# Nine output products two steps earlier, and two of the last four stores from ScalarE

## The chip, the cores and the metric

One of the eight cores of a Trainium2 chip runs the whole kernel. A core has five engines that run at the same time and wait for each other through semaphores: TensorE (PE: matrix products into PSUM, its weight loads shown apart as PEld), VectorE (DVE), ScalarE (ACT), GpSimd (POOL) and SyncE (SP, which here only issues DMA transfers). The metric is the device time of one execution in microseconds (us), as the median of several runs. A profiled execution is timed too; its span runs from its first to its last instruction.

## The reference

The kernel computes a normalised attention block, gated by a small dense network, with a residual:

```
xn = layernorm(x)                       # x: 2048 x 512
s  = attention(xn; wq, wk, wv, wo)      # 32 heads of 16, one shared key and value head
g  = silu(mish(xn @ w1 + b1) @ w2)      # inner width 1792
out = x + s * g

attention: q = xn @ wq, k = xn @ wk, v = xn @ wv
           p = softmax(q k^T / 4);  s = concat_heads(p v) @ wo
```

The part that matters here is the last one: `s` is the product of the heads' outputs (2048 x 512) with `wo` (512 x 512), which is multiplied by `g`, added to `x` and stored.

## The kernel before

**Tiling.** The 2048 rows are cut in 4 chunks of 512. The 32 heads are taken in groups of 4, so there are 8 groups to a chunk and 32 units in all. A unit walks over the 2048 keys in 16 tiles of 128, one tile to a step, so the kernel has NS = 512 steps. In a step TensorE makes four score products (`e`, line 1040, one for each head of the group: 128 keys x 512 rows), ScalarE takes the exponential of each out of PSUM (`pts`, line 1045), and TensorE multiplies those of two steps before with the values (`pv`, line 1127; four to a step, each shown as two instructions in the profile), all into one PSUM bank for the unit. Row maxima of the scores (`m`, lines 1069 and 1073, reduced by VectorE) run 22 steps ahead and end before the stretch that matters here. The products of the dense network and of the projections are slipped in between (`xps`).

**Output products.** For a chunk and a row tile `tt` (0 to 3, 128 rows each) the product with `wo` is a group of 12 matrix products: four tiles of 128 head columns, and three terms for each (high by high, high by low, low by high: numbers are split in two parts for precision). `Group`, `begin`, `finish` and `fill` handle such a group: `begin` takes the first one of the queue that is ready and gives it a PSUM bank, and `fill(n)` issues up to n of its products. In the last chunk each group is cut in two by `wo_groups`: the first 9 products need the head columns 0 to 383 alone, the last 3 need the columns of the last two units. The first parts of row tiles 0, 1 and 2 become ready 16 steps before the end and are issued in the steps from `NS - LEAD` to `NS - 2`, which `tail_block` writes in pairs. The first part of row tile 3 becomes ready at step NS.

**The end.** The main loop writes steps 510 and 511 in this order: four `e`, then `fill(4, ...)`, then the `pv` of step s - 2. At s = NS it writes the `pv` of steps 510 and 511 and calls `o_last`. That function copies the last unit's result out of PSUM (`os`, half by ScalarE on line 1190, half by VectorE on line 1191), turns it with four small products (`low` and `otop`, lines 1197 and 1198), divides by the softmax sums (`sc` on ScalarE, `oc` on VectorE) and writes the last head columns as high and low part into `ot_all`, in two halves: the first half (row tiles 0 and 1) by VectorE, the second (row tiles 2 and 3) by ScalarE on line 1206 and GpSimd. It calls `fill(2, True)` between the copies and the turns, and `fill(7, True)` behind the turns. Then come the four second parts of 3 products each. `post` multiplies each row tile by the gate (`y` or `wop`, VectorE, line 169) and adds `x` (`xr`: GpSimd for row tiles 0 and 1, VectorE for 2 and 3, once all four have been multiplied). `store` issues the 256 KB row tile to memory (line 919).

**Banks.** PSUM has 8 banks of 128 x 512. The pool `ps_e` has three of them, `ps_m` three, `ps_v` one and `ps_x` one. In the last six steps three of the four `e` of a step live in `ps_e` and one in `ps_m`; the PSUM tile of row tile 3 (`wop3`) lives in `ps_e` too. A tile of a pool waits until the bank that it takes over has been read.

The lines that set when the last row tile's first part starts, and where it is issued:

```
first.append(Group(mms[:9], ..., [lambda: NS - (16, 16, 16, 0)[tt], lambda: ot_done.get((c, 2))], ...))
...
for i in range(4):
    e_one(s, i)
fill(4, cur["g"] is not None and cur["g"].alloc is not None)
```

Of the kernel before, what the change touches and what calls it, by code (L numbers as in the profile page):

```python
# [122 lines left out]
def block_kernel(ctx: ExitStack, tc: tile.TileContext, x, wq, wk, wv, wo, w1, b1, w2, out):  # L123
# [10 lines left out]
    pe, act, dve, pool, sp = nc.tensor, nc.scalar, nc.vector, nc.gpsimd, nc.sync  # L134
# [18 lines left out]
    def sp_at(us):  # L153

        sp_t[0] = max(sp_t[0], us_of(step[0])) + us
        return step_of(sp_t[0] + 2.6) - 1

    def pool_at(margin):
        t = step_of(busy[0]) + margin
        return max(t + 0.5 if lead else math.ceil(2 * t) / 2, step[0])  # L160
# [5 lines left out]
    def ew(eng, o, a, b, op):  # L166
        if eng is pool:
            charge(1.3)
        eng.tensor_tensor(out=o, in0=a, in1=b, op=op)  # L169
# [4 lines left out]
    def mul(eng, o, a, b):  # L174
        ew(eng, o, a, b, ALU.mult)
# [32 lines left out]
    outr = out.rearrange("o (t p) d -> (o t) p d", p=P)  # L208
# [24 lines left out]
    def stats(t):  # L233
        st = sb.tile([P, 6], F32, tag="st", name=f"st{t}")
        dve.bn_stats(st, xin[divmod(t, 4)])
        dve.bn_aggr(mvs[:, t], st)
# [153 lines left out]
    def at(s, fn):  # L390
        if s <= step[0]:
            fn()
        else:
            timed.setdefault(s, []).append(fn)
# [37 lines left out]
    def item(tag, key, src):  # L432
        i = Item(tag, key, src)
        items[tag].append(i)
        return i
# [210 lines left out]
    def mm12(lhs, rhs, n):  # L646
        res = []
        tot = 3 * n
        for j in range(n):
            for a, b in TERMS:  # L650
                res.append(Mm(pe, lambda j=j, a=a: lhs(j, a), lambda j=j, b=b: rhs(j, b), len(res), tot))
        return res
# [103 lines left out]
    def hold(hist):  # L756
        hist.append(None)
        n = len(hist) - 1

        def free():  # L760
            hist[n] = pool_at(0.1)
        return free
# [132 lines left out]
    ot_done = {}  # L895
# [3 lines left out]
    def wo_groups(c):  # L899
        last = c == NC - 1  # L900
        its = [item("wb", ("o", k), wo[P * k:P * (k + 1), :]) for k in range(4)]
        first, second = [], []
        adds = []

        def mk(tt):
            st = {}
            t = 4 * c + tt

            def pre():
                if xr_hist[-4] is None:  # L910
                    return False
                st["x"] = sb.tile([P, D], F32, tag="xr", name=f"xr{t}", bufs=4)
                st["free"] = hold(xr_hist)
                sp_at(0.5)
                sp.dma_start(st["x"], xr[t])
                return True

            def store():
                sp.dma_start(outr[t], st["x"])
                st["free"]()  # L920

            def post(ps):
                y = y_of[tt]
                wo_left[c] -= 1
                xx = st["x"]
                if last and tt > 1:
                    mul(dve, ps, ps, y)
                    adds.append(lambda: (ew(dve, xx, ps, xx, ALU.add), store()))
                    if tt == 3:
                        for add in adds:  # L930
                            add()
                    return
                mul(dve, y, ps, y)
                ew(pool, xx, xx, y, ALU.add)
                at(step[0] if last else pool_at(0.1), store)

            mms = mm12(lambda j, a: ot_of[c, j][:, a, P * tt:P * (tt + 1)],
                       lambda j, b: its[j].tile[:, b], 4)
            done = [lambda: ot_done.get((c, 3)), lambda: y_done.get((c, tt))]
            if not last:  # L940
                first.append(Group(mms, post, its, done, pre, wo=c))
                first[-1].dve = True
                return
            kept = {}

            def alloc():
                pool_, tag = ((ps_m, "m"), (ps_x, "x"), (ps_m, "m"), (ps_e, "e"))[tt]
                kept["ps"] = pool_.tile([P, D], F32, tag=tag, name=f"wop{tt}")
                return kept["ps"]
            first.append(Group(mms[:9], lambda ps: None, its, [lambda: NS - (16, 16, 16, 0)[tt], lambda: ot_done.get((c, 2))], wo=c, alloc=alloc))  # L950
            second.append(Group(mms[9:], post, its, done, pre, wo=c, alloc=lambda: kept["ps"]))
        for tt in range(4):
            mk(tt)
        return first + second
# [258 lines left out]
    NS = 16 * NU  # L1213
# [32 lines left out]
    def task(eng, us, fn, deps=(), **kw):  # L1246
        t = Task(eng, us, fn, deps, **kw)
        plan[eng].append(t)
        return t
# [53 lines left out]
    st = [task("DVE", 0.83, lambda t=t: stats(t), at=xat[t], prio=t // 4 * 2) for t in range(12)]  # L1303
# [368 lines left out]
```

## Time and profile before

| | |
|---|---|
| median of 3 runs | 1575.29 us (1574.7 to 1577.19) |
| profiled execution, its time | 1576.59 us |
| profiled execution, its span | 1574.8 us |
| granted TensorE clock, mean | 0.998 |
| busy: PE, DVE, ACT, POOL | 99%, 86%, 82%, 40% of the span |
| DMA queue that the kernel's transfers use | one (SP issues all of them) |

The busy share of TensorE is that of pipelined products whose ends are modelled, so 99% does not say that nothing more fits. The change touches only the last 20 us of the span, from about 1556 us on, and there the engines are far from evenly busy. Such a stretch is read from the order in time of each engine, not from shares.

### The profile page before, as it was taken

To read this page: it belongs to the slowest core of one execution; us is meant where nothing else is said; L and a number is where in the kernel's file an instruction comes from. 1 tells how busy PE (TensorE), PEld (TensorE's weight loads), DVE (VectorE), ACT (ScalarE), POOL (GpSimd) and SP (SyncE) were. 2 spreads that over 40 slices of the span, in tenths; PEclk is the share of its full clock that TensorE was granted. 3 is DMA by queue.
4 is the path that set the end of the run, shared out by engine and by line. 5 is a ranking of instruction groups with operands and counts; after the bars stand their busy time and mean duration, and the time that the engine had idled before them with its cause. 6 is when DMAs were issued, how large, how long until landed. Compare 5 with 4: busy or idle time off the path is not lost.

```text
span 1574.8 us, 31440 instructions
## 1 busy us (share of the span) xinstructions
PE 1560.2 (99%) x11738; PEld 881.1 (56%) x11738; DVE 1348.0 (86%) x2281; ACT 1291.4 (82%) x2502; POOL 636.9 (40%) x669
## 2 busy tenths in 40 slices
PE   9999999999999999999999999999999999999998
PEld 6555655655555565565555556556555555655644
DVE  6998888888989988888898988888889999888843
ACT  5589888788898778977989888897788978888785
POOL 4688249457257202431624422163152323315022
PEclk9999999999999999999999999999999999999999
DMA  6333133133151313203113220322321213031110
GB/s 185 108 125 118 37 103 135 49 112 118 29 158 62 98 27 112 71 18 103 53 46 121 91 92 17 103 68 81 99 59 53 85 58 116 16 98 32 61 36 27
DMA packets 74119, 125.21 MB, mean 80 GB/s; under 512 B 21536, under 2 KB 35648, under 8 KB 73968
## 3 DMA queue, kind: packets, MB, share of 16 engines
q1 hardware_dynamic: 73968, 123.21, 24.9%
q8 instruction: 93, 1.52, 0.4%
q14 instruction: 58, 0.48, 0.1%
HBM read 75.31 MB, written 26.21 MB: 64 GB/s over the span
## 4 chain that ended last, share of the span: by engine, by line
PE 96%; ACT 2%; DVE 1%; DMA 0%; POOL 0%; issue 0%; DVEq 0%; POOLq 0%; ACTq 0%
PE xps L116 43%; PE pv L1127 32%; PE m L1069 12%; PE e L1040 6%; PE xps L112 1%; ACT pts L1045 1%; DVE mb L1073 1%; PE warm L1293 1%; PE kp L335 1%; PE xp L294 0%; PE warm L1372 0%; PE wop L116 0%; DMA rawwb<-in_dram 0%; PE wop L112 0%; DMA ks<-ks 0%
## 5 line engine op out<-in xcount | busy, mean ns | idle before, releaser
L1073 DVE TENSOR_REDUCE mb<-m 128x1 f32<-128x512 f32 x2048 | 1265.8, 682 | 172.2 <-PE m L1069 127.0
L1045 ACT ACTIVATE pts<-e 128x512 f32<-128x512 f32 x2038 | 1060.9, 607 | 222.5 <-PE e L1040 156.2
L1069 PE MATMUL m<-ks,qt 48*128 48x512 f32 (+1 forms) x2048 | 841.8, 425 | 1.6 <-DMA ks<-ks 1.1
L1040 PE MATMUL e<-qt,ks 64*128 64x512 f32 x2048 | 750.1, 407 | 1.8 <-ACT pts L1045 1.5
L1127 PE MATMUL pv<-pts,vaug 128*32 128x512 f32 x4076 | 530.1, 603 | 0.0
L1069 PEld LDWEIGHTS m<-ks,qt 48*128 48x128 f32 (+1 forms) x2048 | 367.3, 185 | 108.1 <-DVE mb L1073 54.6
L1040 PEld LDWEIGHTS e<-qt,ks 64*128 64x128 f32 x2048 | 373.7, 186 | 25.3 <-ACT pts L1045 12.2
L116 PE MATMUL xps<-wbs,act 64*128 64x512 f32 x1248 | 315.3, 397 | 0.0
L116 PE MATMUL xps<-xt,ws 64*128 64x512 f32 x1128 | 313.1, 410 | 0.3 <-ACT pts L1045 0.3
L116 PEld LDWEIGHTS xps<-xt,ws 64*128 64x128 f32 x1128 | 194.5, 185 | 183.3 <-ACT pts L1045 121.4
L116 PEld LDWEIGHTS xps<-wbs,act 64*128 64x128 f32 x1248 | 225.8, 185 | 66.0 <-ACT pts L1045 32.7
L1127 PEld LDWEIGHTS pv<-pts,vaug 128*32 128x32 f32 x4076 | 88.1, 108 | 152.1 <-issue 144.1
L169 POOL TENSOR_TENSOR hb<-hb,t 128x512 f32<-128x512 f32 x56 | 72.1, 1288 | 162.3 <-ACT t L798 82.0
L179 POOL TENSOR_SCALAR t<-t 128x512 f32<-128x512 f32 x56 | 34.4, 615 | 180.2 <-ACT t L785 180.1
L116 PE MATMUL xps<-xt,wq 64*128 64x512 f32 x336 | 93.0, 409 | 0.0
L116 PEld LDWEIGHTS xps<-xt,wq 64*128 64x128 f32 x336 | 57.9, 185 | 55.1 <-ACT pts L1045 37.7
L169 POOL TENSOR_TENSOR oc<-oc,sc 128x512 f32<-128x512 f32 (+1 forms) x16 | 20.6, 1286 | 152.5 <-DMA qt<-qh 78.6
L116 PE MATMUL xps<-wbs,ot_all 64*128 64x512 f32 x288 | 79.5, 408 | 0.0
L116 PEld LDWEIGHTS xps<-wbs,ot_all 64*128 64x128 f32 x288 | 49.5, 184 | 46.7 <-ACT pts L1045 28.5
L169 POOL TENSOR_TENSOR act<-hb,act 128x512 fp32r<-128x512 f32 x56 | 72.2, 1289 | 4.7
L169 POOL TENSOR_TENSOR hb<-hb,u 128x512 f32<-128x512 f32 x56 | 72.2, 1289 | 4.4
L169 POOL TENSOR_TENSOR u<-u,t 128x512 f32<-128x512 f32 x56 | 71.9, 1284 | 4.7
(154 smaller groups left out, 908.6 us busy)
## 6 DMA issues: line engine op xcount, KB each, us to landing
wbs<-w SPq DMA_DIRECT2D x38, 512.0 KB
ws<-w SPq DMA_DIRECT2D x35, 512.0 KB
qt<-qh SPq DMA_DIRECT2D x256, 32.0 KB
w<-wbs SPq DMA_DIRECT2D x14, 512.0 KB
wq<-wq SPq DMA_DIRECT2D x14, 512.0 KB
wbs<-wo SPq DMA_DIRECT2D x12, 512.0 KB
w<-ws SPq DMA_DIRECT2D x11, 512.0 KB
rawws<-in_dram SPq DMA_DIRECT2D x21, 256.0 KB
```

What stands on the lines that cost most here:

```text
L112: self.pe.matmul(ps, self.lhs(), self.rhs(), start=(self.k == 0), stop=(self.k == self.tot - 1))
L116: i = self.pe.matmul(ps, self.lhs()[o], self.rhs()[o], start=(self.k == 0 and self.halves == 0), stop=(self.k == self.tot - 1 and self.hal ...
L169: eng.tensor_tensor(out=o, in0=a, in1=b, op=op)
L179: pool.tensor_scalar(o, o, lim, 0.0, op0=ALU.min, op1=ALU.max)
L335: pe.matmul(kp_of[c][o:o + HALF, 0:z.stop - z.start], w, x_[:, z], start=(dt + i == 0), stop=(dt == 3 and i == len(terms) - 1))
L1040: pe.matmul(e, ks[o:o + 64, P * k:P * (k + 1)], q[o:o + 64, p], start=True, stop=True)
L1045: x = act.activation(dst, e, AF.Exp, scale=0.25)
L1069: pe.matmul(m, q[o, p, P * t:P * (t + 1)], ks[o, C * kb:C * (kb + 1)], start=True, stop=True)
L1073: return dve.reduce_max(out=mb_of[v][:, kb, z:z + 1], in_=m, axis=AX.X)
L1127: pe.matmul(o[32 * j:32 * j + 32], vaug[:, k], pt, start=(k == 0), stop=(k == 15))
L1293: pe.matmul(warm, qts[0][:, 0, 0:P], qts[0][:, 0], start=True, stop=True)
```

## The change

Two numbers and one queue are changed. The first nine products of the last chunk's row tile 3 become ready at step NS - 2 instead of NS. The `fill(4, ...)` of steps 510 and 511 then finds them: it issues four in each, and the ninth is issued by `fill(2, True)` in `o_last`, whose `fill(7, True)` finds nothing any more. The PSUM bank of `wop3` is taken at step 510, behind that step's `e`. And of the last chunk's four stores, those of row tiles 1 and 3 are issued by ScalarE instead of SP.

```diff
             def store():
-                sp.dma_start(outr[t], st["x"])
+                (act if last and tt % 2 else sp).dma_start(outr[t], st["x"])
                 st["free"]()
...
-            first.append(Group(mms[:9], lambda ps: None, its, [lambda: NS - (16, 16, 16, 0)[tt], lambda: ot_done.get((c, 2))], wo=c, alloc=alloc))
+            first.append(Group(mms[:9], lambda ps: None, its, [lambda: NS - (16, 16, 16, 2)[tt], lambda: ot_done.get((c, 2))], wo=c, alloc=alloc))
```

On TensorE, from the last two `e` of step 510 to the end of the program (`e31_14_...` and `e31_15_...` are the scores of steps 510 and 511, `wop0` to `wop3` the row tiles' output products; `x4` counts instructions that read alike):

```order
 L1040 MATMUL e31_14_1_0_21223<-qt1_78,ks_92 128x512
 L1040 MATMUL e31_14_1_1_21226<-qt1_78,ks_92 128x512
+L112 MATMUL wop3_21229<-wbs_101,ot_all_103 128x512 x4
 L1127 MATMUL pv31_20975<-pts_102,vaug_94 32x512 x4
-L1040 MATMUL e31_15_0_0_21233<-qt1_78,ks_92 128x512
-L1040 MATMUL e31_15_0_1_21236<-qt1_78,ks_92 128x512
-L1040 MATMUL e31_15_1_0_21239<-qt1_78,ks_92 128x512
-L1040 MATMUL e31_15_1_1_21242<-qt1_78,ks_92 128x512
+L1040 MATMUL e31_15_0_0_21238<-qt1_78,ks_92 128x512
+L1040 MATMUL e31_15_0_1_21241<-qt1_78,ks_92 128x512
+L1040 MATMUL e31_15_1_0_21244<-qt1_78,ks_92 128x512
+L1040 MATMUL e31_15_1_1_21247<-qt1_78,ks_92 128x512
```

Four products of row tile 3 now stand between the scores of step 510 and the value products of step 508, and so ahead of the scores of step 511 as well; the scores themselves are the same instructions under new buffer numbers. The next piece of the same difference, on TensorE behind the scores of step 511:

```order
+L112 MATMUL wop3_21229<-wbs_101,ot_all_103 128x512 x4
 L1127 MATMUL pv31_20975<-pts_102,vaug_94 32x512 x12
-L112 MATMUL wop3_21261<-wbs_101,ot_all_103 128x512 x2
-L1197 MATMUL low0_21264<-os31_21257,turns_20929 64x256
-L1198 MATMUL otop0_21266<-os31_21257,turns_20929 64x256
-L1197 MATMUL low1_21265<-os2_21258,turns_20929 64x256
-L1198 MATMUL otop1_21267<-os2_21258,turns_20929 64x256
-L112 MATMUL wop3_21261<-wbs_101,ot_all_103 128x512 x7
+L112 MATMUL wop3_21229<-wbs_101,ot_all_103 128x512
+L1197 MATMUL low0_21271<-os31_21266,turns_20929 64x256
+L1198 MATMUL otop0_21273<-os31_21266,turns_20929 64x256
```

Another four stand ahead of the twelve value products of steps 509 to 511, one is left between them and the turns, and the seven behind the turns are gone, so that the second parts of the four row tiles follow the turns directly. On ScalarE, the end of its program in the changed kernel, with what each instruction waits for:

```order
L1202 ACTIVATE sc_20920<-sc_20920 64x256 [waits Activation_49]
L1201 ACTIVATE sc_20920<-low_21272 64x256 [waits PE_49]
L1202 ACTIVATE sc_20920<-sc_20920 64x256 [waits Activation_49]
L1206 ACTIVATE ot_all<-oc_20919 64x256 [waits DVE_49]
L919 DMA out_dram<-xr_20709 128x512 [waits Pool_49]
L919 DMA out_dram<-xr_20932 128x512 [waits DVE_49]
```

The two stores stand behind ScalarE's last computation; SP keeps those of row tiles 0 and 2.

## The prediction

> **What bounds the kernel now.** I read the page's head first, then the chain that ended last for the stretch that the diff touches, then TensorE, ScalarE, the other engines and the store queue in order of time.
>
> ```profile
> span 1574.8 us, 31440 instructions
> PE 96%; ACT 2%; DVE 1%; DMA 0%; POOL 0%; issue 0%; DVEq 0%; POOLq 0%; ACTq 0%
> ```
>
> TensorE carries the chain for nearly all of the span, so every product that is put in its way counts, unless TensorE would have waited there anyway. The change reaches only what lies behind the scores of step 510. There the chain runs:
>
> ```profile
> 1556.67 1.00 PE pv L1127 x8
> 1557.67 1.43 PE e L1040 x4
> 1559.10 2.71 PE pv L1127 x24
> ...
> 1564.40 2.50 PE wop L112 x10
> 1566.90 0.02 issue
> 1566.93 1.37 DVE y L169 x2
> ```
>
> The seven products of row tile 3 that stand behind the turns lie on it: of the ten `wop` from 1564.40, seven are theirs. So do the value products ahead of them. TensorE is therefore the bound on both sides of the move, and the question is at which place it has more idle time.
>
> **The old place.** TensorE, then the engines that make the last head columns:
>
> ```profile
> 1561.74 0.73 PE L112 MATMUL wop<-wbs,ot_all 128*128 128x512 f32 x2
> 1562.49 0.62 PE L1197 MATMUL low<-os,turns 128*64 128x256 f32 x2
> 1564.33 4.60 PE L112 MATMUL wop<-wbs,ot_all 128*128 128x512 f32 x19
> 1561.96 0.38 ACT L1190 ACTIVATE os<-pv 128x256 f32<-128x256 f32 x1 [1.45 <-PE pv L1127]
> 1564.46 0.29 DVE L1208 CAST ot_all<-oc 64x256 fp32r<-64x256 f32 x1
> 1564.78 0.42 DVE L169 TENSOR_TENSOR ot_all<-oc,ot_all 64x256 fp32r<-64x256 f32 x1
> 1565.58 0.41 ACT L1206 ACTIVATE ot_all<-oc 64x256 fp32r<-64x256 f32 x1 [0.75 <-DVE oc L169]
> 1566.14 0.73 POOL L169 TENSOR_TENSOR ot_all<-oc,ot_all 64x256 fp32r<-64x256 f32 x1 [19.46 <-ACT ot_all L1206]
> 1566.93 1.37 DVE L169 TENSOR_TENSOR y<-wop,y 128x512 f32<-128x512 f32 x2 [1.38 <-PE wop L112]
> ```
>
> The two products at 1561.74 lie beside the copy of `os`: the turns wait for its end (1562.34) and start at 1562.49. They cost nothing there. The seven of the x19 group do. Its spacing: a product that stands alone behind another kind takes 0.34 to the next (0.73 for two, less the 0.39 that the last one lasts), and the rest of the 4.60 is 17 gaps of 0.228. So the first product of row tile 0's second part started at 1564.33 + 0.34 + 6 x 0.228 = 1566.04. Its operands were there at 1564.75 (high part) and 1565.20 (low part, needed by its third product). TensorE was up to 1.2 us late.
>
> **What taking the seven away gives.** I keep the old times of the turns and shift everything later. Row tile 0: products at 1564.80, 1565.14, 1565.37. Its third came at 1566.49 and VectorE's product with the gate at 1566.93, 0.44 behind; now 1565.81. Row tile 1's third product follows 0.68 later. Row tile 2's third needs GpSimd's low part (1566.87), so it starts at 1566.92 and VectorE has it at 1567.36; row tile 3 follows 0.68 behind. So VectorE is ahead by 1.12 us at the start and by 0.93 at its third product (1568.29 before). Now the adds and the stores, in order of time and with the transfer engines' share:
>
> ```profile
> 1567.76 2.52 POOL L169 TENSOR_TENSOR xr<-xr,y 128x512 f32<-128x512 f32 x2 [0.89 <-DVE y L169]
> 1568.29 1.38 DVE L169 TENSOR_TENSOR wop<-wop,y 128x512 f32<-128x512 f32 x2
> 1569.58 1.28 DVE L169 TENSOR_TENSOR xr<-wop,xr 128x512 f32<-128x512 f32 x2
> 1569.09 2.04 SPq L919 DMA_DIRECT2D out_dram<-xr  x3
> 1570.31 0.82 SPq L919 DMA_DIRECT2D out_dram<-xr  x2
> 1570.74 0.88 SPq L919 DMA_DIRECT2D out_dram<-xr  x2
> 1571.00:1571.25 0.25, 0.00 (x0) 0.00 (x0) 0.00 (x0) 0.00 (x0) 0.00 (x0) 1.00 0.39 147
> 1571.25:1573.00 1.75, 0.00 (x0) 0.00 (x0) 0.00 (x0) 0.00 (x0) 0.00 (x0) 1.00 1.02 380
> 1573.00:1573.25 0.25, 0.00 (x0) 0.00 (x0) 0.00 (x0) 0.00 (x0) 0.00 (x0) 1.00 0.88 328
> 1573.25:1573.50 0.25, 0.00 (x0) 0.00 (x0) 0.00 (x0) 0.00 (x0) 0.00 (x0) 1.00 0.04 8
> ```
>
> In the last four rows the last two columns are the share of the DMA engines and GB/s. SP issues the second store at 1570.31, the third at 1570.74, the last at about 1571.2. Data of these three begin at 1571.15 (0.39 of a quarter before 1571.25), 0.84 behind the second store's issue, and run without a pause at share 1.02 to 1573.25: 2.10 us, 0.70 a store. So the end hangs on the start of the second store plus 2.10, not on SP's queue.
>
> Now: GpSimd is free at 1566.87, adds from 1566.93 to 1569.45 (2.52), and the second store goes out at 1569.48, 0.83 earlier than before. VectorE's adds start 1.29 behind its third product (1568.29 to 1569.58), at 1568.65, and end at 1569.33 and 1569.93. With two queues the third store can go out on SP at 1569.36, ahead of the second on ScalarE; data run from 1570.20 to 1572.30, 0.95 earlier than 1573.25; I take 0.93, VectorE's lead. On SP alone the order would be second, third, fourth, from 1569.48: 0.83. **The two stores on ScalarE are thus worth 0.10 us, the seven products 0.83.** No row here shows a transfer issued by ScalarE. The nearest are SP's, above all its first of all, issued at 0.74:
>
> ```profile
> 0.74 1.81 SPq L227 DMA_DIRECT2D pts<-in_dram  x4
> 1.60:1.80 0.20, 0.00 (x0) 0.00 (x0) 0.20 (x1) 0.20 (x1) 0.20 (x1) 1.00 0.17 41
> ```
>
> Its data began at about 1.77 (0.17 of 0.20 before 1.80), a lag of 1.03 instead of 0.84. With 1.03 ScalarE's second-tile store is ready at 1570.51, while the third still occupies the engines until 1570.90: free. Bounds: a gain of 0.10, and a loss of 0.19 if that longer lag ended up ahead of all three stores' data. I take the gain.
>
> The Trainium skill prices a transfer differently ("DMA: Bandwidth & Descriptors", section "Anatomy of one DMA", a fit made on transfers that GpSimd issues): about 2.0 us fixed plus bytes over 436 GB/s, so that each store would end on its own clock. By it the last store's issue (1571.2 before, 1569.96 now) would count and the gain be 1.24, the total 1576.7; the share of 1.02 above speaks for the engines being full instead.
>
> **The new place.** TensorE and ScalarE around steps 510 and 511:
>
> ```profile
> 1555.95 0.73 PE L1040 MATMUL e<-qt,ks 64*128 64x512 f32 x4
> 1556.61 1.06 PE L1127 MATMUL pv<-pts,vaug 128*32 128x512 f32 x8
> 1557.60 1.50 PE L1040 MATMUL e<-qt,ks 64*128 64x512 f32 x4
> 1559.03 2.78 PE L1127 MATMUL pv<-pts,vaug 128*32 128x512 f32 x24
> 1556.49 4.03 ACT L1045 ACTIVATE pts<-e 128x512 f32<-128x512 f32 x8 [0.64 <-PE e L1040]
> 1558.12 0.18 PEld L1040 LDWEIGHTS e<-qt,ks 64*128 64x128 f32 x1 [0.31 <-ACT pts L1045]
> 1558.60 0.18 PEld L1040 LDWEIGHTS e<-qt,ks 64*128 64x128 f32 x1 [0.30 <-ACT pts L1045]
> 1556.49 0.60 ACT L1045 ACTIVATE pts<-e 128x512 f32<-128x512 f32 x1 [0.64 <-PE e L1040]
> ```
>
> ScalarE's eight exponentials start every 0.49 us ((4.03 - 0.60) / 7), each done 0.60 behind its start. TensorE's third and fourth scores of step 511 wait for the banks that they free: the two PEld rows. That 0.61 is all the idle time that stands here, and eight products want 2 x (0.34 + 3 x 0.228) = 2.05 us. Step by step:
>
> 1. `wop3` takes the bank of step 510's first score, read at 1556.49 + 0.60 = 1557.09. TensorE stood ready for the value products at 1556.61; it now waits until 1557.14 (a bank's next user comes 0.05 behind: third exponential ends at 1558.07, score at 1558.12), and the value products wait in line behind it. Cost 0.53.
> 2. Four products: 1.02, to 1558.16.
> 3. The value products of step 508 as before, 0.99, then step 511's first two scores at 1559.15 instead of 1557.60. ScalarE has run dry at 1556.49 + 3 x 0.49 + 0.60 = 1558.56. Its next exponential starts 0.54 behind the scores (1555.95 to 1556.49), at 1559.69, and is done at 1560.29. With one of three banks held by `wop3`, the third score must take the bank of the first, so it waits until 1560.34, and the fourth behind it. Two scores take 0.33 (0.66 for four from 1555.95 to 1556.61): 1560.67. From first score to the next work that is 1.52, against 1.43 before (1557.60 to 1559.03): the old waits are not used as cover, since a longer one takes their place. Cost 0.09.
> 4. Four more products: 1.02, to 1561.69. The last exponential starts three times 0.49 or so behind 1559.69, and is done before the value products of step 511 need it at about 1563.5.
>
> The sum is 0.53 + 1.02 + 0.09 + 1.02 = **2.66 us later** for the twelve value products and all that follows. The ninth product fits beside the copy of `os`, as two did.
>
> **The total**: +2.66 - 0.83 - 0.10 = +1.73. The profiled execution had a span of 1574.8 and a time of 1576.59, 1.79 us more, and lay 1.30 above the median. On the median: 1575.29 + 1.73 = **1577.0 us**, on the span 1576.5. That is 0.11% slower, within the 0.2% (3.15 us) that about bounds what a measurement of this kernel tells from no change; the three runs themselves lie 2.5 us apart.
>
> **The rivals.**
>
> *Cover for the wait.* If the bank of `wop3` cost nothing, and the idle 0.61 took in as much of the moved products, they would cost 2.05 - 0.61 = 1.44, and the total 1575.29 + 1.44 - 0.93 = 1575.8. For it: two waits of that size are there. Against it: step 3, they only change their place. Chance 0.13.
>
> *All hidden, faster.* If ScalarE paced both steps, all eight products would be free: 1575.29 - 0.93 = 1574.4. Against it: ScalarE stands idle for 1.45 us ahead of `os`, waiting for TensorE (row at 1561.96). Chance 0.06.
>
> *The clock falls, slower.* The new order makes TensorE's work sparse: a wait of 1 us in step 511, then small turns, then a wait of 0.5 for the last head columns (1564.33 to 1564.80). If the granted clock halved there, the twelve last products would come at gaps of 0.68 and 0.456: the last third product at 1564.80 + 0.68 + 10 x 0.456 = 1570.04 instead of 1567.61, VectorE's last product with the gate at 1570.48, the last add 1.21 behind it (as from 1568.97 to the second add at 1570.18), 0.68 long, so to 1572.37, its store issued at 1572.40, data to 1573.94 instead of 1572.30. That is +1.64: 1578.7, just past 0.2%. The clock in the last column but two:
>
> ```profile
> 1573.50:1574.00 0.50, 0.00 (x0) 0.00 (x0) 0.00 (x0) 0.00 (x0) 0.00 (x0) 1.00 0.00 0
> 1574.00:1574.20 0.20, 0.00 (x0) 0.00 (x0) 0.00 (x0) 0.00 (x0) 0.00 (x0) 0.70 0.00 0
> ```
>
> It fell at about 1574.1, 5.1 us after the last product's end at 1568.93 (1564.33 + 4.60), so a pause of 1 us should not do it. The Trainium skill ("TensorE: Matmul & The Clock Gate", part 1) has the clock halved after an idle window of some 3.4 us that runs freely; the fall here agrees with that. It decides if the clock falls before the turns. Chance 0.03.
>
> *ScalarE's store is dear, slower.* The fourth store's data may begin as late as 1570.20 + 1.40 = 1571.60 without moving the end, a lag of 1.64 from its issue at 1569.96; each microsecond more adds one, and 3.1 us would pass 0.2%. No row comes near that: 1.03 is the longest. Chance 0.05.
>
> **How the numbers follow.** The forecast has 0.73. Its own spread is about 1 us either way, from the runs' 2.5 us and from the steps' ends: 2.66 without any gain gives 1578.0, and 1575.8 is the cover's case. One time in ten of it, and most of the two slow rivals, pass 1578.4: slower 0.12. Below 1572.1 no case ends; 0.02 for what I don't see. Same: 0.86. The range reaches from the forecast down past the cover's case and most of the hidden one, and up to the clock's: 1574.8 to 1578.9.
>
> **What would show it.** In the profile after: an idle wait of about 0.5 us ahead of the first `wop` at 1557.1; about 1 us between the second and third score of step 511, released by ScalarE; the value products' x24 group starting near 1561.7; no `wop` between the turns and the second parts; VectorE's first gate product about 1.5 us later than 1566.93; the three last stores' data again without a pause for 2.1 us; the last data at about 1575.0. I am wrong if the x24 group starts before 1561, if ScalarE's stores need more than 1.6 us to their data, or if the granted clock drops ahead of 1570.

## The result

The changed kernel took **1578.31 us** in the median of 12 runs (1575.4 to 1581.1), against 1574.9 us for the kernel before in 12 runs (1572.59 to 1577.19). The ratio is **1.0018, with a 95% interval of 1.001 to 1.0027**: slower by 1.6 to 4.3 us. The ratio itself lies within the 0.2%, the upper end of its interval past it, and the median lies inside the range forecast. The medians alone are 0.22% apart: five of the change's twelve executions had a mean granted clock of 0.999 or 1.0 and took 1575.4 to 1575.8 us, the seven others had 0.996 or 0.997 and took 1578.06 to 1581.1, so the median is one of the slower seven.

The profiled executions seem to say the opposite: the one after the change has a span of 1574.0 us, the one before 1574.8. The copies of each unit's result (line 1136, first and last start) show where these two part, first of the kernel before, then after the change:

```profile
L1136 ACT ACTIVATE os<-pv x31: 597/598/609, 138.4 to 1526.2; 128x512 f32<-128x512 f32 x31
```

```profile
L1136 ACT ACTIVATE os<-pv x31: 597/597/609, 135.6 to 1523.3; 128x512 f32<-128x512 f32 x31
```

The execution before the change is 2.8 us later at 138 us, and 2.9 us later at 1526: nothing is added in between, and the two programs are the same there. In the first 40 us its granted clock (last column but two) fell to half for some 7 us, which is 3.4 us of full clock:

```profile
26.00:28.00 2.00, 1.83 (x10) 0.76 (x10) 1.22 (x3) 1.76 (x3) 1.73 (x3) 0.96 0.50 170
28.00:34.00 6.00, 6.00 (x23) 2.84 (x20) 2.95 (x5) 3.39 (x11) 0.68 (x1) 0.50 0.53 173
34.00:36.00 2.00, 2.00 (x11) 1.22 (x9) 0.69 (x2) 0.99 (x5) 0.77 (x2) 0.83 0.19 48
```

That of the execution after the change stood at 1.00 in every 2 us from there to 50 us. So the spans can't be compared to 2 us, but the stretch that was changed can. From here on the **tail** is measured: from the first score of step 510 to the end of the span. The page gives a span to 0.1 us only; the trace holds it to the nanosecond (1574.771 before, 1574.009 after), and the tails below are taken from that. Before, it was 1574.77 - 1555.95 = 18.82 us. The expectations further down were written with the rounded spans, so they have 18.85 for it, 20.95 and +2.10 after the change, and 12.31 and 11.45 for the stretch from the first turn on.

TensorE after the change, in order of time:

```profile
1553.05 0.73 PE L1040 MATMUL e<-qt,ks 64*128 64x512 f32 x4
1554.24 1.20 PE L112 MATMUL wop<-wbs,ot_all 128*128 128x512 f32 x4 [0.46 <-ACT pts L1045]
1555.37 1.07 PE L1127 MATMUL pv<-pts,vaug 128*32 128x512 f32 x8
1556.36 0.49 PE L1040 MATMUL e<-qt,ks 64*128 64x512 f32 x2
1557.54 0.50 PE L1040 MATMUL e<-qt,ks 64*128 64x512 f32 x2 [0.68 <-ACT pts L1045]
1557.97 1.19 PE L112 MATMUL wop<-wbs,ot_all 128*128 128x512 f32 x4
1559.10 2.78 PE L1127 MATMUL pv<-pts,vaug 128*32 128x512 f32 x24
1562.55 0.62 PE L1197 MATMUL low<-os,turns 128*64 128x256 f32 x2 [0.24 <-ACT os L1190]
1564.96 3.24 PE L112 MATMUL wop<-wbs,ot_all 128*128 128x512 f32 x12 [0.50 <-DVE ot_all L1208]
```

The tail is 1574.01 - 1553.05 = **20.96 us, 2.14 more**. Both waits that were forecast stand there: the first four products wait for ScalarE's exponential (0.46 idle), and so does the third score of step 511 (0.68 idle, 1.18 behind the first). The 24 value products start 6.05 us behind the first score, where it was 3.08. From the first turn to the end of the span it is 1574.01 - 1562.55 = 11.46 us instead of 12.28: 0.82 come back there. ScalarE runs dry between the two steps:

```profile
1553.59 2.06 ACT L1045 ACTIVATE pts<-e 128x512 f32<-128x512 f32 x4 [0.64 <-PE e L1040]
1556.89 2.27 ACT L1045 ACTIVATE pts<-e 128x512 f32<-128x512 f32 x4 [1.24 <-PE e L1040]
```

Its eight exponentials, one unbroken row of 4.03 us before, are two rows with 1.24 us of waiting for TensorE between them. At the end, GpSimd's adds and the stores on both queues:

```profile
1567.02 2.51 POOL L169 TENSOR_TENSOR xr<-xr,y 128x512 f32<-128x512 f32 x2
1568.34 1.56 SPq L919 DMA_DIRECT2D out_dram<-xr  x2
1568.85 1.28 DVE L169 TENSOR_TENSOR xr<-wop,xr 128x512 f32<-128x512 f32 x2
1569.56 0.93 ACTq L919 DMA_DIRECT2D out_dram<-xr  x2
```

The store of row tile 2 on SP and that of row tile 1 on ScalarE, seen alone, and then the DMA engines' share (last column but one):

```profile
1569.55 0.34 SPq L919 DMA_DIRECT2D out_dram<-xr  x1
1569.56 0.39 ACTq L919 DMA_DIRECT2D out_dram<-xr  x1
```

```profile
1570.25:1570.50 0.25, 0.00 (x0) 0.00 (x0) 0.00 (x0) 0.00 (x0) 0.00 (x0) 1.00 0.39 147
1570.50:1572.25 1.75, 0.00 (x0) 0.00 (x0) 0.00 (x0) 0.00 (x0) 0.00 (x0) 1.00 1.02 382
1572.25:1572.50 0.25, 0.00 (x0) 0.00 (x0) 0.00 (x0) 0.00 (x0) 0.00 (x0) 1.00 0.86 320
```

The last three stores' data again run without a pause, from 1570.40 to 1572.47. The first of them are those of row tile 2, which SP issued at 1569.55, 0.85 us ahead. ScalarE's first store, issued at 1569.56, has its first data at 1570.73 by the packets of its queue in the trace, while those of SP's store still run.

### The profile page after: what moved, and what is told of

Same layout as the page of the kernel before. It is cut to its first block, busy times and chain, and to the rows that moved or that the text cites. A ratio compares the mean times of both kernels' runs of the same rounds, so it can differ in the third digit from the quotient of the medians.

```text
span 1574.0 us, 31438 instructions
## 1 busy us (share of the span) xinstructions
PE 1557.0 (99%) x11738; PEld 879.1 (56%) x11738; DVE 1347.9 (86%) x2281; ACT 1291.3 (82%) x2502; POOL 636.9 (40%) x669
## 4 chain that ended last, share of the span: by engine, by line
PE 96%; ACT 2%; DVE 1%; DMA 0%; issue 0%; POOL 0%; DVEq 0%; POOLq 0%; ACTq 0%
PE xps L116 43%; PE pv L1127 32%; PE m L1069 11%; PE e L1040 6%; ACT pts L1045 1%; PE xps L112 1%; DVE mb L1073 1%; PE warm L1293 1%; PE kp L335 0%; PE xp L294 0%; PE wop L112 0%; PE warm L1372 0%; DMA rawwb<-in_dram 0%; PE wop L116 0%; DMA ks<-ks 0%
```

## The experiments

The theory: a taken score bank and the products behind it delay the value products by 2.97 us; taking the products from behind the turns gives 0.82 back; ScalarE's stores are worth next to nothing. Rivals were put to each part. All are read by the tail, and by the **lead**, from the first score of step 510 to the first of the 24 value products. "No bank held" means no score bank.

| run | lead, us | first turn to end, us | tail, us |
|---|---|---|---|
| before | 3.08 | 12.28 | 18.82 |
| before, again | 3.09 | 12.29 | 18.83 |
| after | 6.05 | 11.46 | 20.96 |
| after, again | 6.05 | 11.45 | 20.96 |
| stores alone | 3.08 | 12.25 | 18.79 |
| products alone | 6.05 | 11.48 | 20.98 |
| all, no bank held | 4.59 | - | - |
| bank asked for early, nothing written, SP alone | 3.07 | 12.29 | 18.81 |
| one step later | 4.28 | 11.46 | 19.19 |
| one product early | 4.20 | 12.04 | 19.70 |
| one product early, no bank held | 3.08 | - | - |
| other order, two queues | 3.07 | 11.35 | 17.88 |
| other order, SP alone | 3.06 | 11.50 | 18.02 |

**Do the executions repeat?** The kernel before, and the one after, without an edit.

> The kernel before, unchanged, once more, to see how far two executions of one program differ, and where. The measure for all runs that follow is the tail: from the first score of step 510 to the end of the span. It was 18.85 us before (1555.95 to 1574.8) and 20.95 after the change (1553.05 to 1574.0). Theory: the tail is set by waits inside the core and comes out at 18.85 within 0.1; what differs between executions lies in the first 50 us, where the profile of before shows the granted clock at 0.50 for about 7 us and the one of after doesn't. Rival: the executions differ all along, then the tail is off by more than 0.3 and the change's +2.10 is not to be trusted.

> The changed kernel once more. Theory: its tail is 20.95 again within 0.1, with the value products at 6.05 and 11.45 from the first turn to the end, whatever the granted clock did in the first 100 us. Rival: the +2.10 was one execution's, then off by more than 0.3.

Both tails came out within 0.01 us of the first ones, and so did the pieces of them in the table. The spans were 1572.8 and 1573.0. The +2.14 (+2.13 between the second pair) is the change's, not an execution's.

**The stores alone.**

```diff
-                sp.dma_start(outr[t], st["x"])
+                (act if last and tt % 2 else sp).dma_start(outr[t], st["x"])
```

> The two stores alone go to ScalarE; the nine products stay where they were. Theory: the three last stores' data already run without a pause and start with the second store, which waits for GpSimd's add; the tail stays at 18.85, at most 0.1 shorter. Rival one: SP's queue of stores was the limit, then the last store is issued 0.3 us earlier (as soon as its add is done) and the tail is 18.5. Rival two: a first transfer from ScalarE is dear, then the tail is over 19.0.

The tail was 18.79, 0.03 to 0.04 shorter than in the two executions of before, and the time the same (ratio 1.0001, 0.9991 to 1.001). SP's queue was not the limit, and a store issued by ScalarE was not dear. The data of the last three stores in this run:

```profile
1566.75:1567.00 0.25, 0.00 (x0) 0.00 (x0) 0.00 (x0) 0.00 (x0) 0.00 (x0) 1.00 0.15 57
1567.00:1567.25 0.25, 0.00 (x0) 0.00 (x0) 0.00 (x0) 0.00 (x0) 0.00 (x0) 1.00 1.00 377
1567.25:1569.00 1.75, 0.00 (x0) 0.00 (x0) 0.00 (x0) 0.00 (x0) 0.00 (x0) 1.00 1.02 380
1569.00:1569.25 0.25, 0.00 (x0) 0.00 (x0) 0.00 (x0) 0.00 (x0) 0.00 (x0) 1.00 0.16 49
```

They take 2.08 us from the first byte to the last, against 2.10 before, whoever issues them.

**The products alone.**

```diff
-[lambda: NS - (16, 16, 16, 0)[tt], ...]
+[lambda: NS - (16, 16, 16, 2)[tt], ...]
```

> The nine products alone move; all four stores stay on SP. Theory: the tail is that of the whole change, 20.95 to 21.05, the value products of step 509 start 6.05 us behind the first score of step 510 (3.08 before), and the stretch from the first turn to the span's end is 11.45 to 11.55 (12.31 before). Rival: the stores on ScalarE gave a good part of that shorter stretch, then it is 11.7 or more and the tail over 21.2.

Tail 20.98, lead 6.05, 11.48 from the first turn on: the whole change, but for 0.02 us. The time was slower by 0.14% (ratio 1.0014, 1.0004 to 1.0024), 2.2 us. The two runs agree: the products make the change, the stores are worth 0.02 to 0.04 us.

**Bank or work?** The same move, but row tile 3 adds into row tile 2's bank, so the kernel no longer keeps the two apart.

```diff
+            if last and tt == 3:
+                mms[0].k = 1
+                mms[9].k = 0
...
+                if tt == 3:
+                    kept["ps"] = wops[2]
+                else:
+                    kept["ps"] = wops[tt] = pool_.tile([P, D], F32, tag=tag, name=f"wop{tt}")
```

> The whole change, but the nine moved products add into row tile 2's PSUM bank instead of taking one of the three score banks; row tiles 2 and 3 of the last chunk thus come out mixed, and the stretch behind the turns, where the two now wait for each other, is not to be compared. What counts is the start of the 24 value products behind step 511, as seen from step 510's first score: 3.08 us before, 6.05 after. Theory: of the 2.97 us the taken bank has about 1.4 (the wait ahead of the first four products and the wait of the third score), and the products 1.5 (2.26 us of work, less the 0.8 in which TensorE would have waited for banks): 4.6 us. Rival: the products cost all of it and the waits only show where TensorE would have stood anyway, then 6.0 again.

```profile
1552.39 0.73 PE L1047 MATMUL e<-qt,ks 64*128 64x512 f32 x4
1553.05 1.21 PE L112 MATMUL wop<-wbs,ot_all 128*128 128x512 f32 x4
1554.20 1.06 PE L1134 MATMUL pv<-pts,vaug 128*32 128x512 f32 x8
1555.19 0.73 PE L1047 MATMUL e<-qt,ks 64*128 64x512 f32 x4
1555.85 1.20 PE L112 MATMUL wop<-wbs,ot_all 128*128 128x512 f32 x4
1556.98 2.78 PE L1134 MATMUL pv<-pts,vaug 128*32 128x512 f32 x24
```

The lead is 4.59, as the theory had it: with a bank of its own out of the way, neither wait is left, and the four scores of step 511 go through in one piece. Of the 2.97 us, 1.46 belong to the bank and 1.51 to the eight products. The bank's part is more than the two waits of the change, because it also takes away cover: the scores of step 511 held TensorE for 1.43 us before (1557.60 to 1559.03), more than half of it waiting, and here for 0.66 (1555.19 to 1555.85), so 0.77 us of the products' work stands where TensorE would have waited; in the change the scores take 1.61 (1556.36 to 1557.97) in spite of the products.

**The bank alone.** This version asks for the bank at step 510 and issues no product there; all four stores are on SP.

```diff
-                fill(4, cur["g"] is not None and cur["g"].alloc is not None)
+                if s == NS - 2 and cur["g"] is None:
+                    begin()
```

> Row tile 3 takes its PSUM bank at step 510, as in the change, but all nine products stay at their old places. The bank's price alone, with no product behind which it could hide. Theory: the third score of step 511 waits for the first one's exponential, which ends 3.06 us behind step 510's first score, so it starts at 3.11 and the 24 value products at 3.54 instead of 3.08; the tail is 18.85 + 0.46 = 19.3. So the bank costs little by itself, and the 1.46 that it has in the change come from the products that push the scores, the exponentials and the third score behind one another. Rival: the bank alone already costs its 1.4 us: 4.5 and 20.3.

Lead 3.07, tail 18.81: nothing changed, and the theory's number was wrong. The edit did not do what it was for. In the built program the four scores of step 511 stand in banks 2, 0, 1 and 4, as before: `wop3` was asked for at bank 2, not written, and the bank was passed on. In the changed kernel `wop3` holds bank 2 and the scores stand in 0, 1, 0 and 4, so the third takes over the bank of the first, as the prediction's third step says. This run thus says nothing on the price of a held bank, and two more were made with one product each.

```diff
-                fill(4, cur["g"] is not None and cur["g"].alloc is not None)
+                if s == NS - 2:
+                    fill(1)
```

> The run that took the bank and issued no product changed no instruction's bank on the scores: a bank is held from the first write on. So now one product, the smallest that holds it: one of the nine at step 510, two beside the copy of the last result, six behind the turns; the stores are those of the change. Theory (a held bank makes waits): the product waits for its bank until 1.19 us behind step 510's first score (TensorE was ready at 0.66), holds TensorE for about 0.45, and the third score of step 511 waits for the exponential of the first, as that has only two banks left beside it; the 24 value products start at 4.25 instead of 3.08, so one moved product costs 1.2 us of the eight products' 2.97. Rival (cost by the product): 3.08 + 2.97 / 8 = 3.5.

> The same one product, but row tile 3 adds into row tile 2's bank (so row tiles 2 and 3 of the last chunk come out mixed, and the stretch behind the turns is not to be compared). Theory: no bank is held, the product fits into the 0.8 us for which TensorE would have waited in step 511, and the value products start at 3.1, as before. Rival: the wait in step 511 is not cover, then 3.5.

TensorE with one product in a bank of its own, and with one in row tile 2's bank:

```profile
1555.87 0.73 PE L1040 MATMUL e<-qt,ks 64*128 64x512 f32 x4
1557.05 0.50 PE L112 MATMUL wop<-wbs,ot_all 128*128 128x512 f32 x1 [0.45 <-ACT pts L1045]
1557.47 1.07 PE L1127 MATMUL pv<-pts,vaug 128*32 128x512 f32 x8
1558.47 0.49 PE L1040 MATMUL e<-qt,ks 64*128 64x512 f32 x2
1559.65 0.49 PE L1040 MATMUL e<-qt,ks 64*128 64x512 f32 x2 [0.68 <-ACT pts L1045]
1560.07 2.78 PE L1127 MATMUL pv<-pts,vaug 128*32 128x512 f32 x24
```

```profile
1554.66 0.73 PE L1047 MATMUL e<-qt,ks 64*128 64x512 f32 x4
1555.33 0.49 PE L112 MATMUL wop<-wbs,ot_all 128*128 128x512 f32 x1
1555.75 1.06 PE L1134 MATMUL pv<-pts,vaug 128*32 128x512 f32 x8
1556.75 1.06 PE L1047 MATMUL e<-qt,ks 64*128 64x512 f32 x4
1557.74 2.78 PE L1134 MATMUL pv<-pts,vaug 128*32 128x512 f32 x24
```

Leads of 4.20 and 3.08, where the theory had 4.25 and 3.1. One product that holds a score bank costs 1.12 us; the same product without it costs nothing, because TensorE would have waited in step 511 anyway (the four scores there take 0.99 us, 1556.75 to 1557.74, against 1.43 before). The 0.46 that the run before this pair forecast for a bank with nothing behind it was not measured. The other seven products add 1.85 us (6.05 - 4.20), 0.26 each.

**One step later.**

```diff
-[lambda: NS - (16, 16, 16, 2)[tt], ...]
+[lambda: NS - (16, 16, 16, 1)[tt], ...]
```

> The products become ready one step later than in the change (step 511): four of them stand behind the scores of step 511, two beside the copy of the last result, three behind the turns. The stores are those of the change. Theory: the bank is taken behind all scores, so no score waits for it; the four products wait for the first exponential of step 511 (ends at 3.06, as TensorE is free) and cost 1.13 and little more: the value products start at 4.24 instead of 3.08 (6.05 in the change). The stretch from the first turn to the end is as short as in the change (11.45), because three products behind the turns still fit ahead of the last head columns. Tail 18.85 + 1.16 - 0.86 = 19.15: still slower than before. Rival: products beside the waits of these steps are free once the bank is out of the way, then 3.1 and a tail of 18.0.

Lead 4.28, tail 19.19. The four products behind the last scores held up no score, and still cost 1.20 us; the gain at the end was 0.82 (11.46 from the first turn), that of the whole move, with three products still standing behind the turns. The gain thus saturates, while the early products cost: the move is a loss at either size.

**The gain without the move.** Steps 510 and 511 as before; the twelve products of row tile 3 are cut in 4, 3 and 5 instead of 9 and 3, and VectorE adds each of its two row tiles right behind its product with the gate. In the first of the two versions ScalarE issues the stores of row tiles 1 and 3.

```diff
-            first.append(Group(mms[:9], lambda ps: None, its, [...], wo=c, alloc=alloc))
-            second.append(Group(mms[9:], post, its, done, pre, wo=c, alloc=lambda: kept["ps"]))
+            n = (9, 9, 9, 4)[tt]
+            first.append(Group(mms[:n], lambda ps: None, its, [...], wo=c, alloc=alloc))
+            if tt == 3:
+                second.insert(2, Group(mms[4:7], lambda ps: None, its, [lambda: ot_done.get((c, 3))], wo=c, alloc=lambda: kept["ps"]))
+                n = 7
+            second.append(Group(mms[n:], post, its, done, pre, wo=c, alloc=lambda: kept["ps"]))
...
-                    adds.append(lambda: (ew(dve, xx, ps, xx, ALU.add), store()))
-                    if tt == 3:
-                        for add in adds:
-                            add()
+                    ew(dve, xx, ps, xx, ALU.add)
+                    store()
```

> A version that takes the gain without the move: steps 510 and 511 as before, and the seven products that stood behind the turns are spread over the places where TensorE waits for the last head columns: two behind the turns, then row tiles 0 and 1, three while GpSimd makes the second half, row tile 2, the last two with row tile 3. VectorE adds x to row tile 2 right behind its product with the gate, and ScalarE issues the stores of row tiles 1 and 3. Theory: the value products start at 3.08 as before; GpSimd's adds start at its own limit, 4.45 us behind the first turn (5.27 before); the last three stores' data start about 1.1 us earlier than before and run without a pause; tail 18.85 - 1.1 = 17.75, 3.2 us shorter than that of the change. The time is 0.07% below before, less than the executions differ. Rival: the second parts of row tiles 2 and 3 come too late for VectorE, and the tail stays at 18.5 or more.

> The version before this one with all four stores on SP. Here row tile 2's add ends ahead of row tile 1's, so SP holds back a store that is ready. Theory: the last three stores' data start with the second store, 0.83 us earlier than before instead of 1.1: tail 18.0, so ScalarE's stores are worth 0.3 us here, where they were worth nothing in the change. Rival: no difference within 0.1.

The first of the two, from the turns on:

```profile
1560.46 0.62 PE L1199 MATMUL low<-os,turns 128*64 128x256 f32 x2
1562.30 4.69 PE L112 MATMUL wop<-wbs,ot_all 128*128 128x512 f32 x19
1563.83 1.39 DVE L169 TENSOR_TENSOR y<-wop,y 128x512 f32<-128x512 f32 x2 [0.31 <-PE wop L112]
1564.93 2.53 POOL L169 TENSOR_TENSOR xr<-xr,y 128x512 f32<-128x512 f32 x2
1565.89 0.70 DVE L169 TENSOR_TENSOR wop<-wop,y 128x512 f32<-128x512 f32 x1 [0.68 <-PE wop L112]
1566.63 0.69 DVE L169 TENSOR_TENSOR xr<-wop,xr 128x512 f32<-128x512 f32 x1
1567.24 0.69 DVE L169 TENSOR_TENSOR wop<-wop,y 128x512 f32<-128x512 f32 x1
```

TensorE's 19 products behind the turns are still there, in 4.69 instead of 4.60 us, but VectorE has row tile 0 at 3.37 us behind the first turn, where it was 4.44 (1566.93 - 1562.49), and GpSimd adds from 4.47 on, its own limit, as in the changed kernel. The tail is **17.88, 0.95 shorter than before and 3.08 shorter than with the change**. The time is 1571.94 us in the median of 12 runs, a ratio of **0.9989 (0.9978 to 0.9999)** to the kernel before. By the tail this version beats both; the time points the same way, but its interval only just leaves out no difference. With all stores on SP the tail is 18.02: ScalarE's two stores are worth 0.15 us here, half of the 0.3 that was expected; the new order of products and adds is worth 0.80. The products' order and the adds' were not run apart. The third store was ready only 0.15 us ahead of the second, since VectorE's add starts 0.74 us behind the product that it reads (1565.89 to 1566.63), not 0.61 as behind an independent one (1566.63 to 1567.24).

## Why the prediction was right

The forecast was 1577.0 us and +1.73; the tail grew by 2.14, and the timed ratio allows 1.6 to 4.3. The mechanism was right in each place, and several terms were a little off.

- **The old place: 0.93 forecast, 0.82 measured** (for the products alone 0.83 and 0.80). VectorE's first product with the gate came 3.38 us behind the first turn (3.32 forecast), its third 4.98 (4.87), GpSimd's adds 4.47 (4.44). What was short is the start of row tile 0's products: 2.41 behind the first turn instead of 2.31, 0.15 behind VectorE's high part and not 0.05. With that, the third store's add ended level with the second's instead of 0.12 ahead.
- **The two stores: 0.10 forecast, 0.03 to 0.04 measured alone and 0.02 on top of the products.** The gain hung on the 0.12 by which the third store was to be ready ahead of the second. The reading that the three last stores fill the DMA engines from the first one's start held in every run. The rival price, by which each store would end by its own issue, would have made the stretch behind the turns 1.24 shorter; it was 0.82. ScalarE's first data came 1.17 us behind their issue (1569.56 to 1570.73), later than the 1.03 that was allowed for, and cost nothing for the reason that the prediction gives: SP's store held the engines meanwhile.
- **The new place, step 1: 0.53 forecast, 0.53 measured** (first product 1.19 us behind the first score in both).
- **Steps 2 and 4, the mis-sized term: 1.02 forecast for four products, 1.13 measured, twice.** The spacing was taken from products among themselves; from the fourth product to the value products, which have another shape, it is 0.32 to 0.33 instead of 0.23, and the rest of the difference is spacings of up to 0.236.
- **Step 3: 0.09 forecast, 0.18 measured.** The wait of the third score was right (1.18, 1.19 forecast). Two scores ahead of the products hold TensorE 0.43, not the 0.33 that half of four scores suggested, again ahead of products of another shape. Sum: 0.53 + 1.13 + 0.18 + 1.13 = 2.97 instead of 2.66.
- **"The old waits are not used as cover"** was right for the change and is not a law: one product without a held bank was fully covered, as the rival of the cover had it. That rival priced the whole move without the bank at 1.44; measured 1.51. That it came so near is in part luck: the products took 2.27 and not 2.05, and the cover was 0.77 and not 0.61 (the idle time of the two PEld rows is less than what the waits add to the scores), and the two errors nearly cancel. It failed on the bank alone.
- **All hidden** fell with the same rows: after the change TensorE, not ScalarE, paced both steps, and ScalarE waited 1.24 us. Before, ScalarE did set the pace of the last two scores of step 511, which is why one product without a bank could hide there.
- **The clock** stayed at 1.00 in the tail. It fell behind the end, between 1572.75 and 1573.00, some 4.6 us after the last product (1564.96 + 3.24 = 1568.20), before the change 5.1 us. In the second execution of the change it fell 2.2 us after it (1567.15 to 1569.35). The Trainium skill's idle window of 3.4 us ("TensorE: Matmul & The Clock Gate", part 1) agrees with the first two and not with the third: of the 3.41 us ahead of that fall TensorE was busy for 1.21. So here the stretch ahead of a fall need not be wholly idle, and the prediction's case against the clock's rival was weaker than it looked, though the clock never fell ahead of the turns.
- **The signs.** One of them, taken as it stands, says that the prediction was wrong: the 24 value products start at 1559.10, and it was to be wrong ahead of 1561. That limit was set in the time of the profile before, and the profile after reached step 510 2.90 us earlier (1553.05 against 1555.95), long ahead of the change. From the first score of step 510, the forecast was 5.74 (1561.69 - 1555.95) and 6.05 was measured, the limit 5.05. A sign that is to be read in another execution has to be a distance from an instruction near the change.
- **The median** lay 1.3 us above the forecast, which had started from 1575.29, 0.39 above the median of 12 runs of the kernel before. So the medians rose by 3.4, the tail by 2.14. Of what lies beyond 1.73, 0.41 is in the terms above; the rest does not stand in the tail, and executions of one program differ by more than that. Tails of one program agreed within 0.01 us, so the tail tests the forecast and the median hardly does.

## What to carry to other kernels

Work moved into an earlier stretch costs more than its own duration when it needs a buffer of a small rotating pool there: one product that held one of three score banks cost 1.12 us, and none when it held nothing. Before moving work to another stage, look for idle time in the stage where it stands: the same products and adds in another order gave the 0.95 us that the move had promised there (0.93), without its cost. And where executions differ by more than the change is worth, measure the stretch that was changed, from a fixed instruction on, not the whole span, and take the span's end as finely as the trace has it.

## What the runs showed of the hardware that was not expected

- A change of product kind on TensorE cost about 0.1 us in each of these places: four products of 128x512 take 1.13 us between products of other shapes, 0.91 within their own stream (4 x 0.228).
- The granted clock can fall to half early in an execution, in some of a program and not in others: in 13 traces not at all in four, for 3.4 us in four and for 6.8 us in five, at 26 to 29 us or near 87. The copy of the first unit's result, at about 135 us, starts the later the longer the fall: at 134.5 to 135.6, 136.4 to 137.0 and 137.5 to 139.0 us. What decides on the fall is not shown; TensorE was busy for 1.11 of the 2 us from 24 us on before the fall in the profile before, and for 1.06 in the one after, which has none.
- ScalarE's queue, which had issued nothing until then, had its first data 1.15 to 1.37 us behind the issue in the six runs with ScalarE's stores that keep the banks apart, SP's stores of the same stretch 0.84 to 0.85. In all six SP's store of row tile 2 was issued up to 0.15 us earlier and its data ran first, so the longer lag cost nothing, and how much of it is the queue's own was not separated.
